# Issuing the output products of an attention and SwiGLU kernel one a slot, from a reserve of three

## The chip, the core and the metric

The kernel runs on one core of one Trainium2 chip. The metric is the device time of one execution in microseconds (us), as the median of several runs. Five engines work side by side, each through its own instructions in order: TensorE (PE, with PEld for its weight loads), VectorE (DVE), ScalarE (ACT), GpSimd (POOL) and SyncE (SP), which issues most of the DMAs.

## The reference

There are 4 batches of 12416 rows with 128 channels, and 32 inducing rows. Attention runs twice: the 32 inducing rows look at all the rows of a batch and give h (32 rows), then every row of x looks at h. The result goes, row by row, through a feed-forward network with an RMS norm and 1536 hidden columns:

```
def mab(q, kv):
    s = scale * (q @ kv.transpose(0, 2, 1))
    s = s - s.max(-1, keepdims=True)
    a = np.exp(s)
    a /= a.sum(-1, keepdims=True) + 1e-09
    return a @ kv
h = mab(I, x)
x = mab(x, h)                      # then reshaped to 49664 rows
...
rms = np.sqrt(np.mean(x * x, axis=-1, keepdims=True) + 1e-06)
xn = x / rms * rms_g
g = xn @ w_gate
silu = g * (1.0 / (1.0 + np.exp(-g)))
val = xn @ w_val
return (silu * val @ w_out).astype(np.float32)
```

## The kernel before

**The work and its unit.** The second attention's result is never formed: its weights a (32 per row) go straight into matmuls with `sg` and `sv`, which hold h times w_gate and w_val (stacked halves in float32r, so one pass each). The feed-forward work is cut into *units*: 25 in a batch, 100 in all, each of up to 512 rows (480 or 256 in the last four of a batch). A unit has 12 *slots*, one for each block of 128 hidden columns. Units and slots are counted from 0. A slot of `ffn` (L535 and after) does this:

- TensorE: g = sg times a (L602), then v = sv times a (L604), each into one of four PSUM banks of the pool `ps_gv`
- ScalarE: silu of g (L606), which frees g's bank
- VectorE: u = silu times v (L608), which frees v's bank. u has 8 buffers (`up`)
- then it calls `slot(j)`, which issues older work, and last it queues its own block's output product.

**Two kinds of output product.** The 12 blocks of a unit are summed into one PSUM bank `acc` (two of them). Eight blocks of a unit take the *plain* product in float32 (L555 with u; two matmul instructions in the trace); they wait in the list `plain`. Blocks 0, 3, 6 and 9 take the *three-pass* product in float32r instead: u is split into factors by ScalarE (L589, and L594 one slot later) and GpSimd (L590, and L595 one slot later), and then `project3` issues three matmuls (L568 and L570 into the bank `u3`, L555 into `acc`). These wait in the list `kara`, each with the slot number from which its factors are expected to be ready; a planner (L784 to L796) works this number out ahead, with a slot assumed to last 1.25 us. It is mostly five slots after the block. It also leaves the three-pass form out around certain slots.

**What closes a unit.** After the last three-pass product ScalarE copies `u3` to o (L573). After a unit's last product of all VectorE adds `acc` to o (L560) and transposes it (L561); two slots later SyncE issues the four DMAs of the store (L582).

**What else stands in the slots.** `schedule(b)` lays the preparation of the next batch over the slots by numbers: loads, transposes on VectorE (L283), scores (L300), sums (L357) and two long exponentials on ScalarE (L329, L416). The two slots of the exponentials (134 and 254 of the 300 in a batch: slot 2 of units 11 and 21) are the *marks* (L755; batch 0 has one more for itself, L730). `seam` prepares the weights a of the next 512 by 4 rows, and `gather` loads a for the next unit at slot 2.

**What sets the order around the change.** Within `slot(j)`: due steps first, then the output products. The number that can be issued is `count`: the plain ones but the newest, and the three-pass ones whose slot has come. In the three slots ahead of a mark (and in slots 2 to 9 of the run) products are held back unless four can be issued. Else up to two are issued, a ready three-pass product first:

```
count = max(len(plain) - 1, 0) + sum(at <= now for at, _ in kara)
hold = k in held or any(k < e <= k + LAG - 2 for e in marks)
if hold and count < LAG - 1:
    return
for _ in range(min(count, 2)):
    if kara and kara[0][0] <= now:
        kara.pop(0)[1]()
    else:
        plain.pop(0)()
```

The PSUM banks of `ps_gv` go to new tiles in the order in which the building of the program expects them free, so a v usually takes the bank of the v two slots back, but in some slots that of the g one slot back.

Of the kernel before, what the change touches and what calls it, by code (L numbers as in the profile page):

```python
# [20 lines left out]
LAG = 5  # L21
# [3 lines left out]
def kernel(  # L25
# [71 lines left out]

    KJ = range(0, NJ - 2, 3)
    NK = len(KJ)
    SLOT, SPLIT = 1.25, 2.9  # L100

    def pool(name, bufs, **kw):
        return ctx.enter_context(tc.tile_pool(name=name, bufs=bufs, **kw))
# [409 lines left out]
    def gather(b, u):  # L513

        s, q = units[u]
        w = per2[s] * m
        hi, lo = split_of[b, s]
        a = moving[b, u] = astk.tile([P, 512], F32R, name="a")
        for k, half in enumerate((hi, lo, hi, lo)):
            queue = nc.scalar if (b, u) == (0, 0) and k % 2 else nc.sync  # L520
            queue.dma_start(out=a[ts(k, m), 0:w].bitcast(F32), in_=half[ts(q, m), 0:w].bitcast(F32))
# [8 lines left out]
    def split_wo():  # L530
# [8 lines left out]
        for k, name in enumerate(("hi", "lo", "d")):  # L539
            kws[name] = xnp.tile([P, 4, 512], F32R, name=f"xn{full - 4 + k}")  # L540

    def ffn(b, u, slot):

        s, q = units[u]
# [55 lines left out]
        for j in range(NJ):  # L600
            g = ps_gv.tile([P, 512], F32, name="gv", tag="gv")
            nc.tensor.matmul(g[:, 0:T], sg[:, ts(j, P)], a[:, 0:T], start=True, stop=True)  # L602
            v = ps_gv.tile([P, 512], F32, name="gv", tag="gv")
            nc.tensor.matmul(v[:, 0:T], sv[:, ts(j, P)], a[:, 0:T], start=True, stop=True)  # L604
            sl = silp.tile([P, 512], F32, name="silu")
            nc.scalar.activation(sl[:, 0:T], g[:, 0:T], AF.Silu)  # L606
            t = up.tile([P, 512], F32, name="u")
            nc.vector.tensor_tensor(out=t[:, 0:T], in0=sl[:, 0:T], in1=v[:, 0:T], op=ALU.mult)  # L608
            slot(j)
            if (b, u, j) in ready:  # L610
                soon(1, lambda j=j, t=t: three(j, t))
            else:
                plain.append(lambda j=j, t=t: project(wo[:, j, :], t[:, 0:T]))
# [164 lines left out]
    flat = [(b, u) for b in range(B) for u in range(NU)]  # L778
# [6 lines left out]
    for b, u in flat:  # L785
        plan, marks, busy = plans[b]
        for j in range(NJ):
            k = u * NJ + j
# [9 lines left out]
    for b in range(B):  # L798
        plan, marks, _ = plans[b]
        held = () if b else range(2, 10)  # L800
        for u in range(NU):

            def slot(j):


                k = u * NJ + j
                now = b * NU * NJ + k
                for one in waiting:
                    one[0] -= 1
                for one in [one for one in waiting if not one[0]]:  # L810
                    waiting.remove(one)
                    one[1]()
                for step in plan.get(k, ()):
                    step()
                for step in seams.get((b, u, j), ()):
                    step()
                if j == 2 and (b, u) in after:
                    gather(*after[b, u])
                count = max(len(plain) - 1, 0) + sum(at <= now for at, _ in kara)
                hold = k in held or any(k < e <= k + LAG - 2 for e in marks)  # L820
                if hold and count < LAG - 1:
                    return
                for _ in range(min(count, 2)):
                    if kara and kara[0][0] <= now:
                        kara.pop(0)[1]()
                    else:
                        plain.pop(0)()

            ffn(b, u, slot)
# [34 lines left out]
```

## Time and profile before

| what | value |
|---|---|
| median of 3 runs | 1771.73 us (1768.76 to 1778.36) |
| the profiled execution | 1775.49 us, its span 1773.4 us |
| TensorE, busy | 1710.4 us (96%) |
| VectorE, busy | 1213.1 us (68%) |
| ScalarE, busy | 1122.5 us (63%) |
| GpSimd, busy | 1026.0 us (58%) |
| mean granted TensorE clock | 0.992 |

The profile is of one execution. Busy times of TensorE rest on modelled ends: a matmul's row often reaches over the start of the next one, so distances from start to start tell more than durations. The feed-forward slots begin at 61.4 us and reach to the end of the span; before them lies the first attention of batch 0. The fourth batch begins at about 1378 us and has nothing beside its own units to do.

### The profile page before, as it was taken

The numbers are of one execution on the slowest core, as the hardware profiler recorded it, in microseconds if no ns is written. First come the engines' busy times: TensorE is split into PE (matmuls) and PEld (weight loads), VectorE is DVE, ScalarE is ACT, GpSimd is POOL, SyncE is SP. The second block draws the span as 40 slices with busy tenths as digits, with TensorE's granted clock in tenths as the row PEclk, the third lists the DMA queues.
The fourth block names the chain that finished last, engine by engine and source line by source line (L and its number), as shares of the span: only waits on it lengthen the run. The fifth ranks groups of instructions, "written<-read, shape, count | busy, mean of one in ns | idle before, by whom it ended". The sixth has DMA issues, their size and how long they took to land.

```text
span 1773.4 us, 23241 instructions
## 1 busy us (share of the span) xinstructions
PE 1710.4 (96%) x6791; PEld 1030.0 (58%) x6791; DVE 1213.1 (68%) x2086; ACT 1122.5 (63%) x2052; POOL 1026.0 (58%) x808
## 2 busy tenths in 40 slices
PE   9899999999999999999999999999999999999998
PEld 7545555655565555564556555565556666666665
DVE  5767776667667777667666777666757666666665
ACT  4345666655666666665667666666566676677665
POOL 0325663656476665465646666465546667667764
PEclk9899999999999999999999999999999999999999
DMA  6334433433343232424334314153211111111111
GB/s 240 83 66 72 77 68 72 103 69 70 54 80 61 43 68 45 101 68 90 66 54 80 59 33 82 35 120 76 54 29 29 37 31 36 30 36 33 34 32 26
DMA packets 389358, 112.64 MB, mean 64 GB/s; under 512 B 365136, under 2 KB 369776, under 8 KB 386672
## 3 DMA queue, kind: packets, MB, share of 16 engines
q1 hardware_dynamic: 388944, 111.02, 31.0%
q8 instruction: 54, 0.88, 0.2%
q14 instruction: 72, 0.59, 0.1%
q10 hardware_dynamic: 288, 0.15, 0.0%
HBM read 53.95 MB, written 27.00 MB: 46 GB/s over the span
## 4 chain that ended last, share of the span: by engine, by line
PE 87%; ACT 6%; DVE 2%; issue 2%; DMA 1%; POOL 1%; SPq 0%; ACTq 0%; DVEq 0%; POOLq 0%
PE acc L555 43%; PE gv L604 15%; PE gv L602 14%; PE u L568 4%; PE u L570 4%; ACT silu L606 4%; PE mm L300 2%; PE mm L483 1%; PE mm L357 1%; DVE u L608 1%; DMA xn<-in_x_dram 1%; PE acc L177 1%; ACT L606 0%; PE gv L357 0%; POOL rs L498 0%
## 5 line engine op out<-in xcount | busy, mean ns | idle before, releaser
L608 DVE TENSOR_TENSOR u<-silu,gv 128x512 f32<-128x512 f32 (+2 forms) x1200 | 788.9, 665 | 495.4 <-ACT silu L606 386.8
L606 ACT ACTIVATE silu<-gv 128x512 f32<-128x512 f32 (+2 forms) x1200 | 696.2, 581 | 530.5 <-PE gv L602 383.4
L555 PE MATMUL acc<-u,wo 128*128 128x512 f32 (+2 forms) x1726 | 865.9, 585 | 2.6 <-POOL wo L255 2.0
L602 PE MATMUL gv<-a,sg 128*128 128x512 f32 (+2 forms) x1200 | 798.5, 666 | 11.8 <-ACT silu L606 9.9
L590 POOL TENSOR_TENSOR xn<-u,xn 128x512 fp32r<-128x512 f32 (+2 forms) x337 | 430.1, 1276 | 494.0 <-ACT xn L589 312.3
L604 PE MATMUL gv<-a,sv 128*128 128x512 f32 (+2 forms) x1200 | 480.2, 400 | 22.2 <-ACT silu L606 18.3
L595 POOL TENSOR_TENSOR xn<-hs,xn 128x512 fp32r<-128x512 f32 (+2 forms) x337 | 422.4, 1253 | 28.0 <-POOL xn L590 2.8
L604 PEld LDWEIGHTS gv<-a,sv 128*128 128x128 f32 x1200 | 227.9, 190 | 276.3 <-issue 133.3
L555 PEld LDWEIGHTS acc<-u,wo 128*128 128x128 f32 x1726 | 320.6, 190 | 97.7 <-issue 26.6
L602 PEld LDWEIGHTS gv<-a,sg 128*128 128x128 f32 x1200 | 228.0, 190 | 243.7 <-issue 130.8
L589 ACT ACTIVATE xn<-u 128x512 fp32r<-128x512 f32 (+2 forms) x337 | 207.5, 616 | 64.1 <-DVE u L608 63.7
L594 ACT ACTIVATE hs<-xn 128x512 f32<-128x512 f32 (+2 forms) x337 | 207.6, 616 | 0.0
L568 PE MATMUL u<-xn,xn 128*128 128x512 f32 (+2 forms) x337 | 142.1, 422 | 0.0
L555 PE MATMUL acc<-xn,xn 128*128 128x512 f32 (+2 forms) x337 | 132.0, 392 | 3.2 <-POOL xn L595 3.2
L570 PE MATMUL u<-xn,xn 128*128 128x512 f32 (+2 forms) x337 | 130.5, 387 | 0.0
L498 POOL TENSOR_TENSOR rs<-ms,mhalf 128x16 f32<-128x16 f32 (+2 forms) x28 | 75.6, 2698 | 28.7 <-DVE ms L496 28.7
L568 PEld LDWEIGHTS u<-xn,xn 128*128 128x128 f32 x337 | 63.5, 188 | 22.4 <-issue 15.9
L560 DVE TENSOR_TENSOR o<-acc,o 128x512 f32<-128x512 f32 (+2 forms) x97 | 65.3, 673 | 15.4 <-ACT o L573 6.8
L555 PEld LDWEIGHTS acc<-xn,xn 128*128 128x128 f32 x337 | 63.4, 188 | 18.8 <-POOL xn L595 5.5
L490 POOL TENSOR_TENSOR z<-z,sc 128x512 f32<-128x512 f32 (+2 forms) x27 | 32.2, 1191 | 72.3 <-DVE z L489 50.0
L570 PEld LDWEIGHTS u<-xn,xn 128*128 128x128 f32 x337 | 63.5, 188 | 16.8 <-issue 4.7
L561 DVE STREAM_TRANSPOSE o<-o 128x512 f32<-128x512 f32 (+2 forms) x97 | 67.7, 698 | 3.3
(159 smaller groups left out, 794.1 us busy)
## 6 DMA issues: line engine op xcount, KB each, us to landing
out_dram<-o SPq DMA_DIRECT2D x320, 64.0 KB, 2.0
xT<-in_x_dram SPq DMA_DIRECT2D x60, 256.0 KB, 4.7
xn<-in_x_dram SPq DMA_DIRECT2D x60, 256.0 KB, 4.8
a<-hi SPq DMA_DIRECT2D x160, 64.0 KB, 2.0
a<-lo SPq DMA_DIRECT2D x158, 64.0 KB, 2.0
w<-w SPq DMA_DIRECT2D x22, 256.0 KB, 3.0
xn<-in_x_dram SPq DMA_DIRECT2D x5, 1024.0 KB, 11.3
out_dram<-o SPq DMA_DIRECT2D x64, 60.0 KB, 2.0
```

The source lines that it names most:

```text
L498: nc.gpsimd.tensor_tensor(out=rs, in0=ms, in1=mhalf[rows, 0:n], op=ALU.pow)
L555: nc.tensor.matmul(acc[:, 0:T], lhsT, rhs, start=st["left"] == NJ, stop=st["left"] == 1)
L568: nc.tensor.matmul(ups[:, 0:T], w[:, i, :], hi, start=st["k"] == nk, stop=False)
L570: nc.tensor.matmul(ups[:, 0:T], w[:, NK + i, :], lo, start=False, stop=not st["k"])
L589: nc.scalar.activation(hi, v, AF.Copy, scale=1.0 - 2.0 ** -13)
L590: nc.gpsimd.tensor_tensor(out=lo, in0=v, in1=hi.bitcast(F32), op=ALU.subtract)
L594: nc.scalar.activation(hs[:, 0:T], hi.bitcast(F32), AF.Copy, scale=2.0 ** -12)
L595: nc.gpsimd.tensor_tensor(out=d, in0=hs[:, 0:T], in1=lo.bitcast(F32), op=ALU.subtract)
L602: nc.tensor.matmul(g[:, 0:T], sg[:, ts(j, P)], a[:, 0:T], start=True, stop=True)
L604: nc.tensor.matmul(v[:, 0:T], sv[:, ts(j, P)], a[:, 0:T], start=True, stop=True)
L606: nc.scalar.activation(sl[:, 0:T], g[:, 0:T], AF.Silu)
L608: nc.vector.tensor_tensor(out=t[:, 0:T], in0=sl[:, 0:T], in1=v[:, 0:T], op=ALU.mult)
```

## The change

A slot now issues one product, and a second one only where more than `spare` can be issued. `spare` is 3 (RESERVE), but 1 in the five slots from a mark on and in the last unit. The choice between a three-pass and a plain product is as before, and so are the planner and the held slots.

```
-    SLOT, SPLIT = 1.25, 2.9
+    SLOT, SPLIT, RESERVE = 1.25, 2.9, 3
...
-                for _ in range(min(count, 2)):
+
+                spare = 1 if any(e <= k < e + LAG for e in marks) or (b, u) == flat[-1] else RESERVE
+                for _ in range(min(count, 2 if count > spare else 1)):
```

In the built program the instructions are the same and stand in another order. Of the 1200 slots, 359 issue no product before and 35 after; 20 issue two plain ones before and 26 after; 337 a three-pass and a plain one before and 7 after; 1 issues three in both. The rest issue one.

TensorE, slots 3 to 5 of unit 8 of the fourth batch, before (gv, acc, u and u3 are numbered tiles; u_14828 is the block of slot 1, u_14838 that of slot 2):

```order
L602 MATMUL gv_14856<-a_14692,sg_12092 128x512
L604 MATMUL gv_14858<-a_14692,sv_12093 128x512
L555 MATMUL acc_14812<-u_14828,wo_118 128x512
L602 MATMUL gv_14865<-a_14692,sg_12092 128x512
L604 MATMUL gv_14867<-a_14692,sv_12093 128x512
L602 MATMUL gv_14879<-a_14692,sg_12092 128x512
L604 MATMUL gv_14881<-a_14692,sv_12093 128x512
L568 MATMUL u3_14890<-xn2_1035,xn5_1030 128x512
L570 MATMUL u3_14890<-xn3_1036,xn5_1030 128x512
L555 MATMUL acc_14812<-xn4_1037,xn5_1030 128x512
L555 MATMUL acc_14812<-u_14838,wo_118 128x512
```

and now (tile numbers differ by a few; u_14803 is the last block of the unit before, u_14827 the block of slot 1):

```order
L602 MATMUL gv_14853<-a_14692,sg_12091 128x512
L604 MATMUL gv_14855<-a_14692,sv_12092 128x512
L555 MATMUL acc_14660<-u_14803,wo_118 128x512
L602 MATMUL gv_14864<-a_14692,sg_12091 128x512
L604 MATMUL gv_14866<-a_14692,sv_12092 128x512
L555 MATMUL acc_14811<-u_14827,wo_118 128x512
L602 MATMUL gv_14875<-a_14692,sg_12091 128x512
L604 MATMUL gv_14877<-a_14692,sv_12092 128x512
L568 MATMUL u3_14890<-xn2_1033,xn5_1028 128x512
L570 MATMUL u3_14890<-xn3_1034,xn5_1028 128x512
L555 MATMUL acc_14811<-xn4_1035,xn5_1028 128x512
```

Slot 4 was empty and has a plain product now, slot 5 had two products and has the three-pass one alone; each plain product comes about one slot later than it did.

VectorE at the same place, slots 1 to 5, before (one row L608 for each slot's u):

```order
L608 TENSOR_TENSOR u_14828<-silu_14826,gv_14824 128x512
L608 TENSOR_TENSOR u_14838<-silu_14836,gv_14834 128x512
L560 TENSOR_TENSOR o_14850<-acc_14661,o_14850 128x512
L561 STREAM_TRANSPOSE o_14850<-o_14850 128x512
L608 TENSOR_TENSOR u_14862<-silu_14860,gv_14858 128x512
L608 TENSOR_TENSOR u_14871<-silu_14869,gv_14867 128x512
L608 TENSOR_TENSOR u_14885<-silu_14883,gv_14881 128x512
```

and now:

```order
L608 TENSOR_TENSOR u_14827<-silu_14825,gv_14823 128x512
L608 TENSOR_TENSOR u_14838<-silu_14836,gv_14834 128x512
L608 TENSOR_TENSOR u_14859<-silu_14857,gv_14855 128x512
L560 TENSOR_TENSOR o_14850<-acc_14660,o_14850 128x512
L561 STREAM_TRANSPOSE o_14850<-o_14850 128x512
L608 TENSOR_TENSOR u_14870<-silu_14868,gv_14866 128x512
L608 TENSOR_TENSOR u_14881<-silu_14879,gv_14877 128x512
```

The pair that closes the unit before stood behind the u of slot 2 and stands behind that of slot 3.

TensorE behind the first mark of the second batch, slots 3 to 5 of unit 11, before:

```order
L602 MATMUL gv_6919<-a_6752,sg_3566 128x512
L604 MATMUL gv_6921<-a_6752,sv_3567 128x512
L555 MATMUL acc_6877<-u_6884,wo_118 128x512
L555 MATMUL acc_6877<-u_6892,wo_118 128x512
L602 MATMUL gv_6929<-a_6752,sg_3566 128x512
L604 MATMUL gv_6931<-a_6752,sv_3567 128x512
L555 MATMUL acc_6877<-u_6906,wo_118 128x512
L602 MATMUL gv_6942<-a_6752,sg_3566 128x512
L604 MATMUL gv_6944<-a_6752,sv_3567 128x512
L555 MATMUL acc_6877<-u_6925,wo_118 128x512
```

and now:

```order
L602 MATMUL gv_6916<-a_6751,sg_3565 128x512
L604 MATMUL gv_6918<-a_6751,sv_3566 128x512
L555 MATMUL acc_6715<-u_6874,wo_118 128x512
L555 MATMUL acc_6876<-u_6883,wo_118 128x512
L602 MATMUL gv_6928<-a_6751,sg_3565 128x512
L604 MATMUL gv_6930<-a_6751,sv_3566 128x512
L555 MATMUL acc_6876<-u_6897,wo_118 128x512
L555 MATMUL acc_6876<-u_6905,wo_118 128x512
L602 MATMUL gv_6938<-a_6751,sg_3565 128x512
L604 MATMUL gv_6940<-a_6751,sv_3566 128x512
L555 MATMUL acc_6876<-u_6922,wo_118 128x512
```

Slot 4 has two plain products where it had one.

## The prediction

> **What bounds the kernel now.** I read the page first (engine totals), then the timeline of one 12-slot unit late in the run, where nothing but the feed-forward work is left, then the chain of waits, then the two kinds of place where TensorE stands still.
>
> ```profile
> span 1773.4 us, 23241 instructions
> PE 1710.4 (96%) x6791; PEld 1030.0 (58%) x6791; DVE 1213.1 (68%) x2086; ACT 1122.5 (63%) x2052; POOL 1026.0 (58%) x808
> ```
>
> The 96% cannot be read as "63 us are idle": ends of matmuls are modelled. What counts is the distance from one start to the next. The timeline of TensorE, slots 2 to 5 of unit 8 of the fourth batch, units and slots counted from 0 (start, duration, line, operation):
>
> ```profile
> 1506.67 0.40 PE L602 MATMUL gv<-a,sg 128*128 128x512 f32 x1
> 1506.90 0.40 PE L604 MATMUL gv<-a,sv 128*128 128x512 f32 x1
> 1507.14 0.39 PE L568 MATMUL u<-xn,xn 128*128 128x512 f32 x1
> 1507.37 0.39 PE L570 MATMUL u<-xn,xn 128*128 128x512 f32 x1
> 1507.60 0.40 PE L555 MATMUL acc<-xn,xn 128*128 128x512 f32 x1
> 1507.83 1.02 PE L555 MATMUL acc<-u,wo 128*128 128x512 f32 x2
> 1508.29 0.80 PE L602 MATMUL gv<-a,sg 128*128 128x512 f32 x1
> 1508.93 0.39 PE L604 MATMUL gv<-a,sv 128*128 128x512 f32 x1
> 1509.16 1.02 PE L555 MATMUL acc<-u,wo 128*128 128x512 f32 x2
> 1509.61 0.79 PE L602 MATMUL gv<-a,sg 128*128 128x512 f32 x1
> 1510.25 0.39 PE L604 MATMUL gv<-a,sv 128*128 128x512 f32 x1
> 1510.48 0.39 PE L602 MATMUL gv<-a,sg 128*128 128x512 f32 x1
> 1511.10 0.49 PE L604 MATMUL gv<-a,sv 128*128 128x512 f32 x1 [0.23 <-ACT silu L606]
> 1511.43 0.39 PE L568 MATMUL u<-xn,xn 128*128 128x512 f32 x1
> ```
>
> Prices, start to start. g and v: 1506.90−1506.67 = 0.23 each, 0.46 a slot. A three-pass product K (L568, L570, L555): 1507.83−1507.14 = 0.69. A plain product P: from its start 1507.83 to the next v 1508.93 is 1.10; less the g between, 0.87 (its tail hides inside the "0.80" of that g). So a slot with P lasts 1.33, with K 1.15, with both 2.02, an empty one 0.46. The cycle now, P / empty / K+P, costs 1.33+0.46+2.02 = 3.81; the cycle after, P / P / K, costs 1.33+1.33+1.15 = 3.81. **No TensorE work goes away.** The change can only remove standstills.
>
> The standstill is in the quoted rows: v of slot 5 follows g by 0.62 instead of 0.23, and the K behind it follows v by 0.33 instead of 0.24: together 0.48. The slot ahead (4) is empty, so this v comes 0.85 after the v before it (1510.25 to 1511.10), and it waits for the PSUM bank that silu has just read. ScalarE and VectorE at that place:
>
> ```profile
> 1508.13 0.63 ACT L594 ACTIVATE hs<-xn 128x512 f32<-128x512 f32 x1
> 1508.65 0.60 ACT L573 ACTIVATE o<-u 128x512 f32<-128x512 f32 x1
> 1510.44 0.60 ACT L606 ACTIVATE silu<-gv 128x512 f32<-128x512 f32 x1 [0.71 <-PE gv L602]
> 1509.28 0.69 DVE L560 TENSOR_TENSOR o<-acc,o 128x512 f32<-128x512 f32 x1 [0.32 <-ACT o L573]
> 1510.01 0.71 DVE L561 STREAM_TRANSPOSE o<-o 128x512 f32<-128x512 f32 x1
> 1510.65 1.25 DVE L608 TENSOR_TENSOR u<-silu,gv 128x512 f32<-128x512 f32 x2
> ```
>
> silu of slot 4 ends at 1510.44+0.60 = 1511.04, and v starts 0.06 later. So a v that uses the bank of the previous slot's g must come at least 0.85 after the previous v. An empty slot gives 0.46. How often this happens, from the chain of waits (total, times, longest):
>
> ```profile
> PE gv L604 <- ACT silu L606: 18.3, 82, 0.2
> PE gv L602 <- ACT silu L606: 9.9, 7, 1.8
> ```
>
> 82 times. The 18.3 us understates it, since the modelled end of g covers part of each gap; by starts it is 82 × 0.48 = 39.4 us. The second row is the other kind of place, where the long exponentials hold ScalarE:
>
> ```profile
> 710.64 0.39 PE L604 MATMUL gv<-a,sv 128*128 128x512 f32 x1
> 710.87 1.02 PE L555 MATMUL acc<-u,wo 128*128 128x512 f32 x2
> 711.37 1.28 ACT L606 ACT_TABLE_LOAD   x1
> 712.67 1.78 ACT L606 ACTIVATE silu<-gv 128x512 f32<-128x512 f32 x3
> 713.32 0.50 PE L602 MATMUL gv<-a,sg 128*128 128x512 f32 x1 [1.43 <-ACT silu L606]
> ```
>
> The last product before the pause starts at 710.87 and would let g start 0.46 later, as at 1507.83/1508.29; g starts at 713.32, 2.0 late. That moment is set by ScalarE alone.
>
> **The change, part by part.** *Empty slots filled.* In the built programs 359 of 1200 slots issue no product before, 35 after; the slots with K+P become slots with K alone. A v behind a P slot comes 1.33 after the last v, behind a K slot 1.15, both above 0.85: the 82 waits lose their cause. I let the share of empty slots that stay keep theirs: 39.4 × 35/359 = 3.8, so the gain is **35.6**. If all 35 wait (only 82 of 359 do now), it is 39.4 − 35 × 0.48 = 22.6; at most 39.4.
>
> *Exponential pauses.* Six times (slot 4 of units 11 and 21, behind the two marks of L755 in each of three batches) one more P is issued ahead of the pause. ScalarE sets when the pause ends, so each P put into it is free: 6 × 0.87 = **5.2**. It is work taken from later slots, so it counts once. It fits into the 2.0.
>
> *The clock.* The stretches of the three pauses at the second mark (stretch, length, busy times, granted clock, DMA):
>
> ```profile
> 461.00:475.00 14.00, 12.21 (x38) 6.60 (x37) 7.23 (x15) 10.83 (x14) 2.17 (x3) 1.00 0.38 60
> 888.00:902.00 14.00, 12.21 (x34) 6.49 (x32) 6.41 (x13) 9.70 (x12) 0.93 (x2) 0.88 0.38 61
> 1316.00:1330.90 14.90, 13.11 (x31) 6.61 (x30) 5.82 (x12) 8.93 (x11) 0.72 (x1) 0.77 0.14 24
> ```
>
> Two of three lost clock: 0.12 × 14.0 + 0.23 × 14.9 = 5.1 us. The pause shrinks from 2.0 to 1.1, so I expect fewer of these; between 0 and 5.1 I take **2.5**. The Trainium skill (TensorE: Matmul & The Clock Gate, Part 1) says that the clock halves after an idle window of about 3.4 us; by that alone a 2 us pause costs nothing and this term is 0, which makes the sum 2.5 smaller. The trace does not agree: the clock fell behind pauses of 2.
>
> *What moves on the other engines.* Products now run 3 to 4 slots behind their block (at most 5), where they ran 2 to 3. u has 8 buffers, so u of slot j needs the product of slot j−8, issued by j−3: no wait. K keeps its distance of 5 slots (6 at a few), and those slots hold 1.33+1.33+1.15+1.33+1.33 = 6.47 instead of 1.33+0.46+2.02+1.33+0.46 = 5.60, so GpSimd's two subtractions get more time; cost nothing. VectorE's closing pair (L560, L561) goes from behind u of slot 2 to behind u of slot 3. L560 no longer stands behind L573 on ScalarE (the 0.32 above), but the pair, 1510.65−1509.28 = 1.37, now holds u of slot 4. Its bank is needed by g of slot 7, which comes, counted from v of slot 4, 0.23+0.87 (g of slot 5), +1.15, +1.33 = 3.58 later. u normally starts 0.85 after v and frees the bank by 0.6 more; with the pair ahead 0.85+0.60+1.37 = 2.82. 0.76 in hand: no cost by itself. The store follows the pair on SyncE's queue two slots on, now slot 5, behind the gather of slot 2 as before; its buffer is needed again two units later: nothing.
>
> *New waits.* More v sit one bank behind (238 wait for ScalarE in the built program, 192 before), and 101 of these follow a K slot without other work, which the trace has nowhere. In hand: 1.15 − 0.85 = 0.30. If a whole ScalarE operation stands in front of silu (L594 to L573 above: 0.52), the wait is 0.22; 101 × 0.22 = 22 at worst. At best nothing; it cannot be below nothing, since a wait does not shorten work. I take 2, near the lower end, because at the commonest place (slot 6 of a unit) hs of the block comes behind that silu, not ahead.
>
> Sum: 35.6 + 5.2 + 2.5 − 2 = 41.3, say **41**. The profiled execution took 1775.5 (span 1773.4 and 2.1 around it), 3.8 above the median 1771.7 of three runs; it goes to about 1734, and the median to 1771.7 − 41 = **1731**. Own range of this case: gains from 22.6+5.2 = 28 to 39.4+5.2+5.1 = 50, so 1722 to 1744.
>
> **Rivals.**
>
> *The waits half return (1752).* The 22 us of the K slots come in full: gain 41 − 20 = 21, 1751 or so. For: ScalarE is in order, and L589 in it waits for VectorE's u. Against: the order of L594 above. Chance 0.10.
>
> *VectorE becomes late, slower.* The pair before u of slot 4 has 0.76 in hand. The second and third batch also have transposes of x on it:
>
> ```profile
> 1003.99 0.69 DVE L283 STREAM_TRANSPOSE xT<-xT 128x512 f32<-128x512 f32 x1
> ```
>
> Where two of these stand there too, it is 1.38 − 0.76 = 0.62 late, and g of slot 7 stops. It decides if that happens in nearly every unit: 97 × 0.62 = 60, so 1771.7 − 41 + 60 = 1791. For: VectorE is busy 68%. Against: in the fourth batch there are none (the VectorE rows above show none), and in the others the plan of L737 to L745 puts them on changing slots. It makes the kernel slower from 0.5 us a unit on. Chance 0.05.
>
> *TensorE is not the bound: no change (1772).* VectorE with 1213 us keeps its work, and what TensorE doesn't wait for here it waits for a slot later. This is what the Trainium skill would lead to (Perfetto Trace Analysis, Identifying the Most-Contended Engine): headroom of TensorE is judged by weight loading, here 58%, below VectorE's 68%. Against it: of the fourteen matmuls in the timeline above one waited, the rest follow each other at their own pace, and the 3.81 of a cycle is their sum; VectorE stands idle ahead of L560. Chance 0.05.
>
> *The slots don't fill.* The reserve is drained by the marks and filled late, so most empty slots stay: about 1768. The built order speaks against it (35 left). Chance 0.02.
>
> **How the numbers follow.** The forecast has 0.78, the rivals 0.10, 0.05, 0.05, 0.02. About 0.5%, 9 us, is what a measurement of this kernel can tell from no change. Faster by more: 0.78 + 0.10 = 0.88. Within: 0.05 + 0.02 = 0.07. Slower: 0.05. The range takes the forecast's own 1722 to 1744 with 2 us of spread below, and reaches up over the half-return case: 1720 to 1756.
>
> **What would show it.** In the profile after, the row "PE gv L604 <- ACT silu L606" should fall from 82 times to about 10, and a unit of the fourth batch should last 4 × 3.81 = 15.2, which is 0.5 less than now. Between v and the next v, K slots should show 1.15 and P slots 1.33 with no idle. The pause behind a mark should be 0.9 shorter and the clock 1.00 there. Waits of L604 behind K slots would mean the first rival; L602 waiting for DVE L608 in slot 7 the second; unchanged unit lengths with the 82 waits gone the third. I am wrong outright if the waits vanish and the time doesn't follow within 10 us.

## The result, and the profile after

The changed kernel takes 1716.09 us (median of 4 runs, 1715.44 to 1717.20) where the kernel before takes 1771.70 (4 runs, 1768.76 to 1778.36): a ratio of 0.9682, 95% interval 0.9654 to 0.9709. That is 55.6 us faster. The forecast was 41 us and 1731, the lower end of the range 1720, so the direction was right and the gain larger than the range allowed.

The profiled execution after took 1715.55 us, its span 1713.4 at a mean granted clock of 0.995. Between the two spans lie 60.0 us: the profiled execution of before was 3.8 above its median, that of after 0.5 below its own. Everything that is booked below is booked against these 60.0.

The totals of the page after:

```profile
span 1713.4 us, 23133 instructions
PE 1676.4 (98%) x6791; PEld 1033.1 (60%) x6791; DVE 1203.1 (70%) x2086; ACT 1145.1 (67%) x2052; POOL 1029.4 (60%) x808
```

The counts of matmuls (6791), of VectorE's instructions (2086) and of ScalarE's (2052) are those of before. No work went away, and the span is 60.0 shorter.

The timeline of TensorE from v of slot 4 to v of slot 6 of unit 8 of the fourth batch (start, duration, line, operation; three dots stand for g of slot 6). The prediction's rows of before end at slot 5 of the same unit:

```profile
1457.56 0.39 PE L604 MATMUL gv<-a,sv 128*128 128x512 f32 x1
1457.79 1.02 PE L555 MATMUL acc<-u,wo 128*128 128x512 f32 x2
1458.24 0.79 PE L602 MATMUL gv<-a,sg 128*128 128x512 f32 x1
1458.87 0.39 PE L604 MATMUL gv<-a,sv 128*128 128x512 f32 x1
1459.10 0.40 PE L568 MATMUL u<-xn,xn 128*128 128x512 f32 x1
1459.34 0.39 PE L570 MATMUL u<-xn,xn 128*128 128x512 f32 x1
1459.57 0.39 PE L555 MATMUL acc<-xn,xn 128*128 128x512 f32 x1
...
1460.03 0.40 PE L604 MATMUL gv<-a,sv 128*128 128x512 f32 x1
```

From v to v: 1458.87 − 1457.56 = 1.31 with a plain product between, 1460.03 − 1458.87 = 1.16 with a three-pass product. No row has a wait. The v of slot 5 (1458.87), which stood 0.62 behind its g's start before, stands 0.63 behind it now as well, but for another reason: the g of a slot behind a plain product carries that product's tail, as every such g does, and the three-pass product follows the v by 0.23 instead of 0.33. Two slots of the one kind and one of the other make 2 × 1.31 + 1.16 = 3.78, against the 3.81 that the prediction put together.

VectorE in the same stretch:

```profile
1457.39 0.69 DVE L608 TENSOR_TENSOR u<-silu,gv 128x512 f32<-128x512 f32 x1 [0.81 <-ACT silu L606]
1457.99 0.68 DVE L560 TENSOR_TENSOR o<-acc,o 128x512 f32<-128x512 f32 x1
1458.71 0.71 DVE L561 STREAM_TRANSPOSE o<-o 128x512 f32<-128x512 f32 x1
1459.35 1.25 DVE L608 TENSOR_TENSOR u<-silu,gv 128x512 f32<-128x512 f32 x2
```

The closing pair (L560, L561) stands behind the u of slot 3 now, and two u stand right behind it (x2): those of slots 4 and 5. No matmul waited for them.

The chain of waits (total, times, longest), the same two rows as before:

```profile
PE gv L602 <- ACT silu L606: 5.3, 8, 1.0
PE gv L604 <- ACT silu L606: 1.8, 8, 0.2
```

The v waits fell from 82 to 8; the pauses of g behind the long exponentials have 1.0 as their longest where they had 1.8.

**Where the 60.0 us came from.** I took the start of the first matmul of each of the 1200 slots in both traces, and from each slot's change in length took off the product that it issues more or less in the one kernel than in the other (0.86 for a plain one, 0.40 of it in the slot behind, where its tail shows; 0.69 for a three-pass one). What is left is time in which TensorE stood still or ran at a lower clock:

| place | gain, us |
|---|---|
| 88 slots behind an empty one, whose v stood 0.5 or more behind its g (69 of them slot 5 of a unit), 0.47 each on the mean | 41.0 |
| lower granted clock | 6.9 |
| pauses behind the six marks of the first three batches, beside the clock | 3.2 |
| units 0 to 2 of batch 0 | 2.5 |
| unit 24 (256 rows) of three batches | 2.6 |
| elsewhere | 3.8 |
| sum | 60.0 |

The fourth batch, which has nothing beside its units, gains 12.5 in 25 units. Most of its units of 512 rows without matmuls of `seam` last 15.2 each, where they lasted 15.7; those with them last 15.9, where they lasted 16.7.

### The profile page after: what moved, and what is told of

Same layout as the page of the kernel before. It is cut to its first block, busy times and chain, and to the rows that moved or that the text cites. A ratio compares the mean times of both kernels' runs of the same rounds, so it can differ in the third digit from the quotient of the medians.

```text
span 1713.4 us, 23133 instructions
## 1 busy us (share of the span) xinstructions
PE 1676.4 (98%) x6791; PEld 1033.1 (60%) x6791; DVE 1203.1 (70%) x2086; ACT 1145.1 (67%) x2052; POOL 1029.4 (60%) x808
## 4 chain that ended last, share of the span: by engine, by line
PE 88%; DVE 4%; ACT 4%; issue 2%; POOL 1%; DMA 1%; DVEq 0%; ACTq 0%; POOLq 0%
PE acc L555 43%; PE gv L604 15%; PE gv L602 15%; PE u L568 5%; PE u L570 4%; PE mm L300 2%; DVE u L608 1%; PE mm L483 1%; ACT silu L606 1%; PE mm L357 1%; DMA xn<-in_x_dram 1%; PE acc L177 1%; ACT sc L416 1%; ACT L606 1%; ACT sc L329 0%
## 5 line engine op out<-in xcount | busy, mean ns | idle before, releaser
L608 DVE TENSOR_TENSOR u<-silu,gv 128x512 f32<-128x512 f32 (+2 forms) x1200 | 787.8, 665 | 457.7 <-ACT silu L606 409.0
L602 PE MATMUL gv<-a,sg 128*128 128x512 f32 (+2 forms) x1200 | 788.4, 657 | 7.7 <-ACT silu L606 5.3
L604 PE MATMUL gv<-a,sv 128*128 128x512 f32 (+2 forms) x1200 | 469.4, 391 | 2.9 <-ACT silu L606 1.8
L595 POOL TENSOR_TENSOR xn<-hs,xn 128x512 fp32r<-128x512 f32 (+2 forms) x337 | 422.7, 1254 | 59.7 <-issue 15.9
L604 PEld LDWEIGHTS gv<-a,sv 128*128 128x128 f32 x1200 | 227.3, 189 | 216.0 <-issue 119.7
L561 DVE STREAM_TRANSPOSE o<-o 128x512 f32<-128x512 f32 (+2 forms) x97 | 67.7, 698 | 3.4
L560 DVE TENSOR_TENSOR o<-acc,o 128x512 f32<-128x512 f32 (+2 forms) x97 | 64.7, 667 | 2.6 <-PE acc L555 2.2
```

The source lines that it names most:

```text
L595: nc.gpsimd.tensor_tensor(out=d, in0=hs[:, 0:T], in1=lo.bitcast(F32), op=ALU.subtract)
```

## The experiments

The disputed question is what the 41.0 us are. The prediction held that an empty slot makes the next v wait, so that each empty slot is a cost. But 359 slots were empty and 82 waited, and 69 of the 88 places are the same slot of a unit. There the closing pair stood on VectorE. So the rival theory is that the pair, and not the empty slot alone, makes v wait: the bank of v two slots back is held until u of slot 3 is done, and u of slot 3 stands behind the pair.

**E1. The kernel before, with only the closing pair one slot later.** TensorE's order is that of before, with all its 359 empty slots.

```
-                if nk:
-                    nc.vector.tensor_tensor(out=o[:, 0:T], in0=acc[:, 0:T], in1=o[:, 0:T], op=ALU.add)
-                nc.vector.transpose(out=o[:, 0:T], in_=(o if nk else acc)[:, 0:T])
-                soon(2, lambda: store(o))
+                def close():
+                    (nk and nc.vector.tensor_tensor(out=o[:, 0:T], in0=acc[:, 0:T], in1=o[:, 0:T], op=ALU.add)); nc.vector.transpose(out=o[:, 0:T], in_=(o if nk else acc)[:, 0:T])
+                    soon(2, lambda: store(o))
+                soon(1, close)
```

> The kernel before with its 359 empty slots and every TensorE instruction in its place; only the pair that closes a unit on VectorE (L560, L561) comes one slot later, behind the next u. Theory A, as predicted: a v waits because the slot ahead is empty. Then nothing changes that matters, 1772 within 5 us, and L604 still waits for silu about 82 times. Theory B: the place of the pair decides; u of slot 3 is no longer held, a v behind an empty slot is seldom given the bank of the previous g (26 times instead of 103 in the built program), and about three quarters of the waits go: 0.75 x 39 = 29 us, about 1743.

Measured: 1749.95 us (1749.72 to 1752.13), ratio 0.9878 (0.9864 to 0.9893) against 1771.69 in the same job. That is 21.7 us with every instruction of TensorE, ScalarE and GpSimd in its old order. The banks that v gets change with the place of the pair, as the expectation says, so this run does not part the two. Slots 4 and 5 of unit 8 of the fourth batch:

```profile
1489.94 0.39 PE L604 MATMUL gv<-a,sv 128*128 128x512 f32 x1
1490.17 0.39 PE L602 MATMUL gv<-a,sg 128*128 128x512 f32 x1
1490.40 0.40 PE L604 MATMUL gv<-a,sv 128*128 128x512 f32 x1
```

Slot 4 is empty (its v at 1489.94 is followed by the next g), and v of slot 5 follows its g by 0.23, with no wait. And the chain of waits:

```profile
PE gv L604 <- ACT silu L606: 4.5, 20, 0.2
PE gv L604 <- DVE u L608: 3.7, 7, 0.8
```

20 v wait for silu where 82 did. The theory that an empty slot by itself makes the wait fell. The full 29 us did not come. In six units of the fourth batch (1, 5, 9 and so on) operations of `seam` still stand on VectorE behind the u of slot 2 and hold it: slot 5 of those units gained nothing, that of most others 0.32 to 0.51.

**E2. The kernel before, with two banks for g and two for v.** The four banks can then no longer change places; v always takes the bank of the v two back.

```
-    ps_gv = pool("ps_gv", 4, space=PSUM)
+    ps_gv = pool("ps_gv", 2, space=PSUM); ps_v = pool("ps_v", 2, space=PSUM)
...
-            v = ps_gv.tile([P, 512], F32, name="gv", tag="gv")
+            v = ps_v.tile([P, 512], F32, name="gv", tag="gv")
```

> The kernel before with two PSUM banks for g alone and two for v alone, so that no v ever takes the bank of the g one slot back. If that choice of bank is the whole cause of the 82 waits, they go: 1771.7 - 39, about 1733. If the choice was only the better of two (v of slot 5 would else wait for the u of slot 3, which stands behind the closing pair), the waits stay under the name of VectorE: about 1772, not below 1765, and the PE idle time of L604 is put down to DVE u L608.

Measured: 1843.22 us (1842.04 to 1843.64), ratio 1.0401 (1.0385 to 1.0416): 71.5 slower, which neither theory expected. About 5.2 of it lie in the first attention, which uses the same pool. The rest is the wait that the four banks avoided. The row of the chain of waits, and rows of TensorE and VectorE in unit 5 of the fourth batch, a unit with a seam (L471, L475 and two short rows left out behind them, L483):

```profile
PE gv L604 <- DVE u L608: 79.3, 100, 2.6
```

```profile
1505.81 0.70 DVE L471 STREAM_TRANSPOSE eT<-sc 128x512 f32<-128x512 f32 x1
1506.43 0.65 DVE L475 TENSOR_REDUCE l<-sc 128x16 f32<-128x512 f32 x1
1507.40 0.39 PE L602 MATMUL gv<-a,sg 128*128 128x512 f32 x1
1507.74 0.69 DVE L560 TENSOR_TENSOR o<-acc,o 128x512 f32<-128x512 f32 x1
1508.46 0.71 DVE L561 STREAM_TRANSPOSE o<-o 128x512 f32<-128x512 f32 x1
1509.10 1.25 DVE L608 TENSOR_TENSOR u<-silu,gv 128x512 f32<-128x512 f32 x2
1509.80 0.50 PE L604 MATMUL gv<-a,sv 128*128 128x512 f32 x1 [2.02 <-DVE u L608]
1510.14 1.22 PE L483 MATMUL mm<-eT,gram 128*128 128x512 f32 x2
```

v waits 2.02 us for a u that stands behind the seam's operations and the pair. In units without a seam the wait is shorter: in most of those of the fourth batch v of slot 5 stands 0.86 to 1.16 behind its g, where before it stood 0.62. This is the cause made visible: in the kernel before, v escaped this long wait by taking the bank of the previous slot's g, and paid 0.48 for it. So the free choice of a bank does not cause the standstill, as it may look from the row "L604 <- ACT silu"; it makes a long one short.

**E3. The changed kernel, with one product instead of two in slot 4 behind each mark.** This undoes the part of the change that fills the pauses.

```
-                for _ in range(min(count, 2 if count > spare else 1)):
+                for _ in range(min(count, 2 if count > spare and k - 2 not in marks else 1)):
```

> The changed kernel with one product instead of two in slot 4 behind a mark (the second comes a slot later). If a product put into the pause of the exponentials is free, as predicted, this costs 6 x 0.87 = 5.2 us: 1721, and 1.7 more for each further stretch of halved clock. If the pause does not matter: 1716.

Measured: 1721.74 us (1720.66 to 1722.27), ratio 0.9716 (0.9701 to 0.9730), which is 5.65 above the changed kernel's 1716.09. The number is near the expected one, but what makes it is not the 0.87 for each. By the starts of the slots, the product that is left out costs 0.3 behind each first mark and 0.8 behind each second one, 3 × 0.3 + 3 × 0.8 = 3.3. Between the two profiled executions lie 6.5 us: these 3.3, some 1.7 of clock, and 1.5 in units 0 to 2 of batch 0, where the edit also takes a product out behind the mark that batch 0 has for itself. The stretch of the second mark of batch 0 (stretch, length, busy times of PE, PEld, DVE, ACT, POOL, granted clock, DMA):

```profile
451.00:467.00 16.00, 14.20 (x34) 7.11 (x33) 6.28 (x14) 9.36 (x13) 2.10 (x3) 0.79 0.31 49
```

(1 − 0.79) × 16.00 = 3.4 us of clock are lost there, where the changed kernel lost none (1.00 at this mark, in the rows further down). The changed kernel lost 1.7 at the second mark of batch 1 instead, which this run did not.

**E4. The changed kernel, with units 0 to 2 issued as before.**

```
-                spare = 1 if any(e <= k < e + LAG for e in marks) or (b, u) == flat[-1] else RESERVE
+                spare = 1 if any(e <= k < e + LAG for e in marks) or (b, u) == flat[-1] else 0 if b == 0 and u < 3 else RESERVE
```

> The changed kernel with the old rule in units 0 to 2 of the first batch. The trace of after shows v's follower in slot 11 of unit 0 without the 1.9 us standstill that before had there (a product that waited for its own u, two slots old). If that is a gain of the change, this kernel is 1.8 to 2.5 us slower than the changed one: about 1718. If it was the weights' preparation alone that differed: 1716.

Measured: 1718.19 us (1717.49 to 1718.86), ratio 0.9697 (0.9681 to 0.9714): 2.1 above the changed kernel. The 2.5 us of the start are real. The reason that the expectation gave for them was wrong, though: the traces name another. The output product of unit 0, slot 11, in the kernel before and then in the changed one:

```profile
89.63 1.98 PE L555 MATMUL acc<-u,wo 128*128 128x512 f32 x4 [1.55 <-POOL wo L255]
```

```profile
86.07 1.02 PE L555 MATMUL acc<-u,wo 128*128 128x512 f32 x2
```

Before, two plain products in one slot asked for a piece of `wo` that GpSimd was still preparing (L255). Now the slot issues one, whose piece is ready, and the later piece is asked for later. This alone is 1.8 of the 2.5.

**E5. The changed kernel, with slot 4 left empty.** Slot 2 of a unit always issues two where two are there. Slots 2 to 5 are then as before in most units (the pair behind u of slot 2 in 93 units by the trace), and 123 slots are empty; the other empty slots stay filled.

```
-                for _ in range(min(count, 2 if count > spare else 1)):
+                for _ in range(min(count, 2 if count > spare or j == 2 else 1)):
```

> The changed kernel, but slot 2 of a unit always issues two products. In the steady units that makes slots 2 to 5 what they were before (K+P with the closing pair behind u of slot 2, then P, then an empty slot 4, then K), while the other empty slots stay filled: 123 empty slots in all, against 359 before and 35 in the changed kernel. If every empty slot costs alike, this loses (123-35)/324 of the change's 55 us: 15, about 1731. If only the empty slot behind the closing pair costs, nearly the whole wait is back, 0.49 in each of some 80 units: about 1716 + 40 = 1756.

Measured: 1745.41 us (1744.78 to 1746.26), ratio 0.9842 (0.9815 to 0.9869): 29.3 above the changed kernel. If every empty slot cost alike, the return should have been some 15. By the starts, 29.1 lie in slot 5 of 64 units, 0.45 each on the mean, and next to nothing elsewhere in sum. Slots 4 and 5 of unit 8 of the fourth batch:

```profile
1482.09 0.39 PE L604 MATMUL gv<-a,sv 128*128 128x512 f32 x1
1482.32 0.39 PE L602 MATMUL gv<-a,sg 128*128 128x512 f32 x1
1482.85 0.50 PE L604 MATMUL gv<-a,sv 128*128 128x512 f32 x1
1483.19 0.39 PE L568 MATMUL u<-xn,xn 128*128 128x512 f32 x1
```

It is the picture of before: v 0.53 behind g instead of 0.23, the product 0.34 behind v instead of 0.23, though all the other slots of the unit are filled. The chain of waits shows only 39 places, since the modelled end of g covers most of each gap; the 0.14 that it leaves in the rows above has no row in the chain:

```profile
PE gv L604 <- ACT silu L606: 8.8, 39, 0.2
```

**E6. The changed kernel, with the pair one more slot later** (behind u of slot 4). The edit is that of E1.

> The changed kernel with the closing pair (L560, L561) one slot later still, behind u of slot 4. If the pair's place has stopped to matter once the slots are filled, 1716 within 3 us. If the change gained by putting the pair behind u of slot 3 and nowhere else, some of E1's 22 us is lost again: 1725 or more.

Measured: 1714.12 us (1712.40 to 1714.92), ratio 0.9664 (0.9637 to 0.9691). With slot 4 filled, the place of the pair is worth 2 us or less, where it was worth 21.7 with slot 4 empty.

**E7. The changed kernel, with two banks for g and two for v.** The edit is that of E2.

> The changed kernel with two banks for g and two for v. The kernel before lost 71 us by that, in waits of v for the u two slots back. If filled slots give u the time it needs, only the units where a seam's reductions stand ahead of the closing pair still wait: 24 x about 1 us, 1716 + 24 = 1740 or less. If the free choice of banks matters as much as before: 1716 + 71 = 1787.

Measured: 1751.86 us (1747.32 to 1753.54), ratio 0.9874 (0.9845 to 0.9904): 35.8 above the changed kernel, 6.4 of it in the first attention. Both expectations missed.

```profile
PE gv L604 <- DVE u L608: 23.2, 42, 2.1
```

So the filled order still needs the free choice at 42 places, where the order of before needed it at 100. The 0.76 us in hand of the prediction holds for a unit without other work on VectorE; other units still need a bank from elsewhere, and with four to choose from find one (by the starts, unit 22 alone loses 3.0 in each of three batches once it can't).

**E8. The changed kernel, with a reserve of four.** 25 empty slots stay instead of 35.

```
-    SLOT, SPLIT, RESERVE = 1.25, 2.9, 3
+    SLOT, SPLIT, RESERVE = 1.25, 2.9, 4
```

> The changed kernel with a reserve of four: 25 empty slots instead of 35, the ten being ahead of the marks and in the first units. By 0.48 for each: 1716 - 5 = 1711. If none of these ten was followed by a wait: 1716.

Measured: 1716.20 us (5 runs, 1715.08 to 1717.40), ratio 0.9677 (0.9650 to 0.9704). The ten slots cost nothing that shows when empty. So the empty slots that stay are not 0.48 each either.

**E9. The kernel before, with slots 2 and 3 issuing one product each.** That fills slot 4 in 64 more units and puts the pair behind u of slot 3 in 63; 295 slots stay empty.

```
-                for _ in range(min(count, 2)):
+                for _ in range(min(count, 1 if j in (2, 3) and not any(e <= k < e + LAG for e in marks) else 2)):
```

> The kernel before, but slots 2 and 3 of a unit issue one product each, so that slot 4 of 64 more units has a product (and the closing pair stands behind u of slot 3 there); 295 empty slots stay, those of slots 1, 7 and 10 nearly all. If only the empty slot behind the closing pair costs: 64 waits of 0.48 to 0.5 go, 31 us, about 1740. If every empty slot costs alike: 64 of 324 filled slots, 11 us, about 1760.

Measured: 1750.70 us (1748.89 to 1751.14), ratio 0.9862 (0.9840 to 0.9885), 22.2 below the kernel before (1772.88 in this job). This is halfway between the two expectations. By the starts, slot 5 gains 30.0, 0.47 on the mean in its 64 units, as the theory of the one place says. But slot 3 gives 7.5 back: some 0.12 in each of about 40 units, and 0.87 in unit 16 of three batches, where a matmul of the preparation (L429) waits. Its rows in unit 8 of the fourth batch, from v of slot 2 on:

```profile
1486.96 0.40 PE L604 MATMUL gv<-a,sv 128*128 128x512 f32 x1
...
1487.88 0.40 PE L602 MATMUL gv<-a,sg 128*128 128x512 f32 x1
1488.13 0.50 PE L604 MATMUL gv<-a,sv 128*128 128x512 f32 x1
1488.47 1.02 PE L555 MATMUL acc<-u,wo 128*128 128x512 f32 x2
```

Slot 2 now has the three-pass product alone, and slot 1 ahead of it is empty. v comes 1488.13 − 1486.96 = 1.17 after the v before, and the product 0.34 behind it instead of 0.23: a wait of 0.1 behind a K slot. This looks like the "new wait" of the prediction, though no row names what the v waits for. It is there where an empty slot stands ahead of the K slot, and it was not found in the changed kernel, where the slot ahead is filled.

**E10 and E11. The changed kernel again, and E6 again,** on the same chip, to see whether the 2 us of E6 are real.

> The changed kernel once more, beside E11 on the same chip: 1716.

> E6 once more, beside the changed kernel on the same chip. If its 2 us are real: 1714, with no run above the lowest of the changed kernel. If they were chance: 1716.

Measured: E10 1715.71 us (1715.38 to 1718.49), ratio 0.9672 (0.9652 to 0.9691); E11 1714.61 us (1714.08 to 1715.66), ratio 0.9663 (0.9645 to 0.9681). Seven of the eight runs of E6 and E11 lie below the lowest run of the changed kernel (1715.38). The expectation asked for none above it, and one run of E11 is (1715.66). 1 to 2 us are likely, at the edge of what these runs can tell.

**What the experiments settle.** Most of it was one place in a unit: v of slot 5, if slot 4 is empty and VectorE is held by the pair or by a seam. In the kernel before, slot 4 is empty in 92 units and v of slot 5 waits in 69 of them. In 22 of the other 23 TensorE has matmuls of the next batch's preparation (L300, L357, L429) in slots 2 to 4, which only two of the 69 have; so it seems that these gave VectorE its time, but no run tried it.

The pair one slot later is enough where no seam stands (E1, 22 us). A filled slot 4 was never tried with the pair in its old place: E9 and the changed kernel fill slot 4 and move the pair at once (30 us in slot 5 of E9), and E5 undoes both (29 us). That the filling counts by itself is seen in the units with a seam. In the six of the fourth batch the pair stands behind u of slot 3 in E1 and in the changed kernel alike; with slot 4 empty v stands 0.62 or more behind its g and waits, with slot 4 filled it does not wait (the changed kernel fills other slots too). How the 30 us divide between the two in the other units stays open.

Which units carry the other 19 of the 88 places was read from the starts alone and not tried apart. The other empty slots cost little: the 267 slots behind them gained some 17 us with the change, the clock included, which is 0.06 each, against 0.41 in the 92 slots 5. E8 fills ten more for nothing.

## Why the prediction was right and wrong

The sum of the prediction against the profiled execution, term by term:

| term | forecast | measured | difference |
|---|---|---|---|
| empty slots filled, less new waits | 35.6 − 2 = 33.6 | 41.0 | +7.4 |
| exponential pauses | 5.2 | 3.2 | −2.0 |
| clock | 2.5 | 6.9 | +4.4 |
| units 0 to 2 | none | 2.5 | +2.5 |
| unit 24 | none | 2.6 | +2.6 |
| elsewhere | none | 3.8 | +3.8 |
| sum | 41.3 | 60.0 | +18.7 |

**Right.** "No TensorE work goes away" and "The change can only remove standstills": the count of matmuls is the same and the K slots and P slots have the distances that were worked out (1.16 for 1.15, 1.31 for 1.33). The v waits fell from 82 to 8, as the share of the empty slots that stay had it. The units of the fourth batch went to 15.2 where no seam stands, half a microsecond less. The pair behind u of slot 3 costs nothing there: two u start behind it and no matmul waits. The rivals fell: the row "L604 <- ACT silu" has 8 places in all and none of them was found behind a K slot; TensorE does not wait for VectorE at slot 7; and the time moved by 55.6, so TensorE was the bound. The sentence on contention in the Trainium skill (Perfetto Trace Analysis, Identifying the Most-Contended Engine), which by weight loading (58%), one of its two measures for TensorE, would have named VectorE, led the other way from what was measured here.

**The step that failed** is the sum itself: it was made of two rows of the chain of waits and of the clock at three marks, everything else stood at nothing, and its own range, 1722 to 1744, was bounded by those rows too. The forecast had said that it is wrong outright if the waits vanish and the time doesn't follow within 10 us; it missed by 15. Three things came out larger than the sum had them; the pauses, which came out smaller, are further down.

*"82 times … by starts it is 82 × 0.48 = 39.4 us", less 3.8 and 2.* The price was near: these 82 gained some 36.7, 0.45 each. What the sum left out stands in the same chain of waits before, under another name:

```profile
PE gv L604 <- DVE u L608: 3.6, 8, 0.8
```

Of the 88 places 79 are among the 82, seven are among these eight and gained 5.1, and two have no row and gained nothing. The 3.8 for the empty slots that stay and the 2 for new waits did not come: the ten that E8 fills cost nothing, and E9 shows where a new wait does come and how small it is (0.12).

*"Between 0 and 5.1 I take 2.5" for the clock.* The upper end came from the second marks alone, the only stretches that were looked at. Two stretches of the first batch have the same loss. The windows 130 to 146 and 172 to 188, before:

```profile
130.00:146.00 16.00, 12.92 (x35) 6.89 (x35) 11.29 (x19) 7.34 (x14) 8.98 (x6) 0.89 0.22 41
172.00:188.00 16.00, 13.76 (x46) 7.60 (x45) 10.95 (x20) 7.76 (x16) 7.07 (x6) 0.89 0.42 65
```

and after:

```profile
130.00:146.00 16.00, 12.92 (x41) 7.19 (x40) 12.43 (x21) 8.44 (x16) 10.16 (x8) 1.00 0.31 54
172.00:188.00 16.00, 14.48 (x49) 8.90 (x48) 12.27 (x23) 9.48 (x18) 11.81 (x9) 1.00 0.49 81
```

That is 0.11 × 16.00 × 2 = 3.5 us. At the three second marks the clock after is

```profile
451.00:465.00 14.00, 13.00 (x43) 7.54 (x42) 8.49 (x16) 9.72 (x17) 5.34 (x5) 1.00 0.39 63
863.00:877.00 14.00, 13.00 (x36) 6.99 (x35) 7.18 (x14) 8.76 (x14) 3.74 (x4) 0.88 0.36 56
1275.00:1289.90 14.90, 13.90 (x45) 7.78 (x44) 8.83 (x21) 11.22 (x16) 4.05 (x4) 1.00 0.11 17
```

which loses 0.12 × 14.00 = 1.7 where before lost 5.1. Together 3.5 + 5.1 − 1.7 = 6.9. One such stretch was left in this execution. The profiled execution of the same kernel in E10 was granted 0.993 instead of 0.995 and took 2.9 us longer, so the term is not fixed from run to run.

*Units 0 to 2 and unit 24 were not looked at.* The start has waits for `wo` (E4). The three units of 256 rows gain 2.6; I read this from the starts alone and no run tried it apart.

**The cause was half of it.** The prediction put it so: "The slot ahead (4) is empty, so this v comes 0.85 after the v before it", and "a v that uses the bank of the previous slot's g must come at least 0.85 after the previous v". That is true of the places that wait, but it does not say why only 82 of some 359 wait. The prediction saw the pair on VectorE ahead of u of slot 3, quoted it, and moved it at "no cost by itself". It did not ask what the pair's old place cost. E1 answers: 21.7 us, without one product moved. In the changed kernel the pair and the products moved together, so that trace alone could not have told.

*"Six times … each P put into it is free: 6 × 0.87".* Only in part: slot 4 gains 0.83 at each of the six, but behind the three first marks 0.60 comes back two slots later, which leaves 6 × 0.83 − 3 × 0.60 = 3.2. Unit 11 of batch 0, after, from slot 4 on (TensorE, ScalarE and VectorE; rows between are left out):

```profile
274.80 1.88 PE L555 MATMUL acc<-u,wo 128*128 128x512 f32 x4
276.65 1.78 ACT L606 ACTIVATE silu<-gv 128x512 f32<-128x512 f32 x3
277.30 0.49 PE L602 MATMUL gv<-a,sg 128*128 128x512 f32 x1 [0.62 <-ACT silu L606]
...
279.24 1.84 DVE L608 TENSOR_TENSOR u<-silu,gv 128x512 f32<-128x512 f32 x3
279.94 1.12 PE L555 MATMUL acc<-u,wo 128*128 128x512 f32 x2 [0.32 <-DVE u L608]
```

Two plain products (x4 matmuls) stand in the pause and g waits 0.62 where it waited 1.43 at this kind of place; but at 279.94 a product waits for its own u, one of three that VectorE begins at 279.24, since the stock has been drained. The same was seen in E3, where leaving the product out cost 0.3 behind a first mark and 0.8 behind a second one.

## What to carry to other kernels

Count the standstills by the distances from start to start over all the tiles of a kind, not by one named row of waits, and look once over every stretch that differs (the first tiles, the narrow ones, each dip of the clock) before the sum is bounded. When only some of the places with a feature wait (82 of 359 empty slots), the feature is not the cause yet: look for what those have in common on the other engines, here a closing step that stands in an in-order queue ahead of the operation that frees a buffer. Moving that step by one slot was worth 21.7 us by itself here, and is cheap to try.

## What the runs showed of the hardware

**The clock falls behind some standstills of 1 to 2 us, and costs about 1.7 us at a time.** In E2 a wait of 2.02 us is followed by matmuls at half speed:

```profile
1510.60 1.18 PE L568 MATMUL u<-xn,xn 128*128 128x512 f32 x1
1511.58 0.63 PE L570 MATMUL u<-xn,xn 128*128 128x512 f32 x1
1512.01 0.63 PE L555 MATMUL acc<-xn,xn 128*128 128x512 f32 x1
```

(0.39 or 0.40 elsewhere; 1512.01 − 1511.58 = 0.43 from start to start, where it is 0.23 at full speed; the 1.18 of the first row also holds the tail of the seam's float32 matmul ahead of it, L483) and the window around it is granted 0.83:

```profile
1508.00:1518.00 10.00, 8.20 (x22) 4.85 (x22) 5.40 (x9) 4.27 (x8) 3.89 (x4) 0.83 0.18 26
```

0.17 × 10.00 = 1.7 us lost. The other stretches lose 1.7 (0.12 × 14.00), 1.8 (0.11 × 16.00), or twice that (0.23 × 14.9 = 3.4; 0.21 × 16.00 = 3.4 in E3): multiples of one step. The Trainium skill (TensorE: Matmul & The Clock Gate, Part 1) has a free-running window of about 3.4 us and half the clock after an idle one. By an estimate from the page's figure, one such window at half the clock costs 1.7 us, and the steps above agree with it. That a whole window must be idle does not agree: the standstills here were of about 2 us, and of 1.0 at most in the changed kernel, whose window 863 to 877 is granted 0.88. Not each of them was followed by a slow stretch.

**The time varies with the granted clock.** Over all jobs the kernel before ran from 1767.83 us, at a mean granted clock of 0.995, to 1779.84, at 0.989 (27 runs), and the changed kernel from 1715.38 at 0.995 to 1718.49 at 0.993 (8 runs). That fewer pauses made it steadier is not shown: E2, whose waits are the longest, stayed within 1.6 us in its four runs, at 0.983 to 0.985.

**Four banks that may change places are worth far more than two and two.** 71.5 us in the order of before and 35.8 in the changed one (E2, E7), with 5 to 6 of each in the first attention, at the same number of banks.
